# GpSimd operations that wait for the VectorE operation issued before them, and one PSUM tile for two stages of an attention and mixer kernel

## The chip, the cores and the metric

The kernel runs on one core of a Trainium2 chip. The time is the device time of one execution in microseconds (us). The engines of the core run side by side and are ordered among themselves by semaphores alone: TensorE (PE in the profile; its weight loads are PEld), VectorE (DVE), ScalarE (ACT), GpSimd (POOL) and SyncE (SP), which issues the transfers from and to the memory of the chip.

## What is computed

Rotary attention over 4 batches, 8 heads, 576 positions and a head size of 64, and behind it a token mixer and a channel mixer, all in float32. Cut to what matters:

```python
q_rot, k_rot = rotate(q), rotate(k)            # x1*cos - x2*sin, x1*sin + x2*cos
scores = matmul(q_rot, k_rot^T) / sqrt(64)
attn = exp(scores - max); attn = attn / (sum + 1e-9)
x = (attn @ v) with the heads side by side      # (4, 576, 512)
h = relu(x^T @ w_tok1) @ w_tok2                 # 576 -> 256 -> 576, over the positions
u = x + h^T
out = u + relu(u @ w_ch1) @ w_ch2               # 512 -> 1536 -> 512
```

The weights come as float64 (`moe_w_*`) and are turned on the chip into pairs of a high and a low part, each in the format in which TensorE multiplies fast; a product is then three matmuls (high by high, high by low, low by high).

## The kernel before

**Tasks and orders.** The kernel is written as tasks. `add` makes one: the engine, a cost estimate, a function that issues the instructions, what it depends on, and the buffers that it holds. A task can have alternatives on another engine. `Plan.run` hands the tasks out in one sequence, and each engine executes its own instructions in that sequence. Three calls of `run` follow each other. The first two take their sequence, with the choice of engines, from lists in the file (`ORDER1`: attention, the token weights and the token mixer of the first batch; `ORDER2`: the token mixers of the other three batches, the first transposes and the first group of channel weights). The third (the channel mixer and the remaining weights) makes its sequence by the plan's own clock: `start` estimates when a task could begin, `place` moves the clock and calls the task's function.

**Port tasks.** Some VectorE tasks have `port=True`: those that read two operands from SBUF or run in a fast mode from SBUF to SBUF. These are the steps of `f64_split` (lines 783 to 804: two ScalarE reads, a clamp at L787, a shift at L789, an OR at L791, a mask at L793, a product at L795, a sum at L797, then the high part at L803 and the low part at L804; L787, L795, L797 and L804 can also be GpSimd's), the split of the token mixer's input (`splits`, L865 and L867), and the rotation of the first pair of heads. In `start` the plan lets such a task begin only when its estimate of GpSimd's clock has passed, and in `place` it moves GpSimd's clock to the task's end. That is an estimate alone: no semaphore of the program orders the two engines for it.

**Attention.** The 16 pairs of heads are worked in a pipeline. For each pair (`prep`), GpSimd rotates k and q in three operations each (L470, L472, L476 on `w`, `uk`, `uq`); TensorE transposes the result (L505) and the copies go to `kt` and `qt` (L523). In `pair`, TensorE makes the scores (L649), VectorE takes each row's maximum on the way out of PSUM (L534, into `p`), ScalarE the exponentials (L546), TensorE transposes them (L675), ScalarE and VectorE copy them to `pt` (L685), TensorE multiplies by v (L698); the result goes through `oT` (L701) and a transpose (L727) to `X` (L732, L738), scaled by the reciprocal (L713) of a sum to which GpSimd adds 1e-9 (L710).

**PSUM.** In `attention` all eight banks are one tile `s` (128 x 8 x 512), from a pool that is opened in `attention` and closed behind the first `run`; `Banks` hands out its banks one by one and keeps for each the time at which it is free. `mixers` opens a second pool with eight tiles of one bank, `m0` to `m7`, and hands them out through `Slots`, all free at time 0.0. The second pool lies where the first one lay.

**Mixers.** `tokens` multiplies the split input by the token weights (L893), applies the ReLU and splits it (L898, L901), multiplies again (L915) and adds to `X` or its tails `XT` (L918). `splits` has two buffers `xs`, each freed by the L893 matmuls that read it. `up` transposes the result (L984) and splits it (L989, L990); `cm1` is the first channel product (L1010, L1012, L1014), `cm2` the second (L1037, L1039), in four groups of channel weights.

Of the kernel before, what the change touches and what calls it, by code (L numbers as in the profile page):

```python
# [9 lines left out]
F32 = mybir.dt.float32  # L10
# [5 lines left out]
PSUM = bass.MemoryType.PSUM  # L16
# [6 lines left out]
class Slots:  # L23


    def __init__(self, tiles, fifo=True):
        self.free = [(0.0, i, t) for i, t in enumerate(tiles)]
        self.fifo = fifo
        self.made = 0
        self.taken = 0  # L30
# [56 lines left out]
class Plan:  # L87


    def __init__(self):  # L90
        self.tasks = []
        self.made = 0
        self.given = False
        self.clock = {e: 0.7 for e in LAG}
        self.slack = SLACK
        self.mode = None

    def add(self, eng, dur, fn, deps=(), bufs=(), prio=0.0, alts=(), mode="full", port=False):
        t = Task()
        t.mode = mode  # L100
        t.port = port
        t.alts = [(eng, dur, fn)] + list(alts)
        t.deps = [d for d in deps if d is not None]
        t.bufs = list(dict.fromkeys(getattr(b, "buf", b) for b in bufs))
        for b in t.bufs:
            b.users += 1
        t.prio = prio
        t.end = None
        t.n = self.made = self.made + 1
        t.heirs = []  # L110
        self.tasks.append(t)
        return t
# [28 lines left out]
    def place(self, t, s, eng, dur, fn):  # L141
        end = s + dur
        for b in t.bufs:
            if b.held is None and isinstance(b.slots, Banks):
                sl = b.slots
                c = sl.pick(sl.free, b.two, self.clock["PE"])
                for i in c[1]:
                    del sl.free[i]
                i = c[1][0]
                b.held = (c[0], c[1], sl.tile[:, i:i + 2] if b.two else sl.tile[:, i])  # L150
            if b.held is None:
                b.held = min(b.slots.free)
                b.slots.free.remove(b.held)
                b.slots.taken += 1
        if fn:
            fn()
        else:
            end = -1e9
        t.end, t.eng = end, eng
        if eng == "PE":  # L160
            self.mode = t.mode
        self.clock[eng] = max(self.clock[eng], end)
        if eng == "DVE" and t.port:
            self.clock["POOL"] = max(self.clock["POOL"], end)
        for b in t.bufs:
            b.users -= 1
            b.end = max(b.end, end + LAG[eng])
            if not b.users and isinstance(b.slots, Banks):
                b.slots.free.update((i, b.end) for i in b.held[1])
            elif not b.users:  # L170
                b.slots.free.append((b.end,) + b.held[1:])
# [165 lines left out]
def rope_attention_mixer_kernel(ctx: ExitStack, tc: tile.TileContext, q, k, v, w_tok1, w_tok2, w_ch1, w_ch2, tab, out):  # L337
# [16 lines left out]
    NP = B * H // 2  # L354
    HP = H // 2
    P = 128
    plan = Plan()
    add = plan.add

    const = ctx.enter_context(tc.tile_pool(name="const", bufs=1))  # L360
    ident = const.tile([P, P], F32, name="ident")
    X = [const.tile([P, R, DM], F32, name=f"X{b}") for b in range(B)]
    XT = [const.tile([P, DM], F32, name=f"XT{c}") for c in range(B // 2)]
# [10 lines left out]

    def attention(ctx):
        pers = ctx.enter_context(tc.tile_pool(name="pers", bufs=1))
        psum = ctx.enter_context(tc.tile_pool(name="psum", bufs=1, space=PSUM))

        def slots(nm, n, shape, dt=F32, pool=pers, fifo=True):
            return Slots([pool.tile(shape, dt, name=f"{nm}{i}") for i in range(n)], fifo)  # L380
# [13 lines left out]
        lts = slots("lt", 2, [P, 4])  # L394
        rts = slots("rt", 2, [P, 4])
        nms = slots("nm", 8, [P, 2])
        banks = Banks(psum.tile([P, 8, 512], F32, name="s"), 8)

        for r0, r1 in ((0, 2), (2, R)):
            nc.scalar.dma_start(out=tabs[:, :, r0:r1], in_=tab[0:2, :, r0:r1].rearrange("a p r d -> p a r d"))  # L400
# [426 lines left out]
    def tok_weights(places):  # L827
        same = lambda x: x
        w1v = w_tok1[0:M, :].rearrange("(p r) f -> p (r f)", r=R)
        for i in range(2):  # L830
            pr = next(places)
            sb, t = stage(0, w1v[:, i * 512:(i + 1) * 512], pr)
            w1_done.extend(f64_split((sb, 512), [(w1h[:, 2 * i:2 * i + 2].rearrange("p r f -> p (r f)"),
                                                  w1l[:, 2 * i:2 * i + 2].rearrange("p r f -> p (r f)"), same)], [t], pr))
        pr = next(places)
        sb, t = stage(0, w_tok1[M:S, :], pr)
        _, t2 = stage(0, w_tok1[M:S, :], pr, o=1, sb=sb)
        w1_done.extend(f64_split((sb, FT), [(w1th, w1tl, same)], [t, t2], pr))
        for a in range(2):
            pr = next(places)  # L840
            sb, t = stage(0, w_tok2[a * P:(a + 1) * P, 0:M], pr)
            w2_done.extend(f64_split((sb, M), [(w2h[:, a, 0:M].rearrange("p (r s) -> p r s", r=R),
                                                w2l[:, a, 0:M].rearrange("p (r s) -> p r s", r=R),
                                                lambda x: x.rearrange("p (s r) -> p r s", r=R))], [t], pr))
        pr = next(places)
        sb, t = stage(0, w_tok2[0:P, M:S], pr)
        _, t2 = stage(TL, w_tok2[P:2 * P, M:S], pr, sb=sb)
        w2_done.extend(f64_split((sb, 2 * TL), [(w2h[:, :, M:S], w2l[:, :, M:S],
                                                 lambda x: x.rearrange("p (a s) -> p a s", a=2))], [t, t2], pr))
# [9 lines left out]
    def splits(b, rows, px):  # L859
        for r in rows:  # L860
            xb = Buf(xss if r < R else xts)
            src = X[b][:, r] if r < R else tail_of(b)
            hi = (lambda xb=xb: xb.t[:, 0]) if r < R else (lambda xb=xb: xb.t[0:TL])
            lo = (lambda xb=xb: xb.t[:, 1]) if r < R else (lambda xb=xb: xb.t[TL:P])
            c = lambda e, hi=hi, src=src: lambda: (e.copy if e is nc.scalar else e.tensor_copy)(out=hi(), in_=src)  # L865
            x = add("ACT", act(DM, True), c(nc.scalar), x_done[b], [xb], px, port=True, alts=[("DVE", dve2(DM), c(nc.vector))])
            f = lambda e, hi=hi, lo=lo, src=src: lambda: e.tensor_tensor(out=lo(), in0=src, in1=hi(), op=ALU.subtract)  # L867
            y = add("DVE", dve(DM), f(nc.vector), [x], [xb], px, port=True, alts=[("POOL", pool(DM), f(nc.gpsimd))] if r < R else [])
            split[b, r] = (xb, [x, y])
# [52 lines left out]
    KC = DM // P  # L922
    KF = FC // P

    def mixers(ctx):
        plan.slack = {"PE": 0.11, "ACT": 0, "DVE": 0, "POOL": 0, "SP": 0.18}
        wc = ctx.enter_context(tc.tile_pool(name="wc", bufs=1))
        psum = ctx.enter_context(tc.tile_pool(name="psum2", bufs=1, space=PSUM))
        m_ps = Slots([psum.tile([P, 512], F32, name=f"m{i}") for i in range(8)], False)
        FG = 3  # L930
        N = 4 * P
        W = FG * P
# [145 lines left out]
    with tc.manual_schedule():  # L1078
        with ExitStack() as c:
            banks = attention(c)  # L1080
            tok_weights(iter(AT["tok"]))
            for b in range(EARLY):
                tokens(b, banks)
            splits(EARLY, range(PRE), 9 * 4 * (EARLY + 1) + AT["pre"][0])
            for r in range(PRE):
                split[EARLY, r][0].users += 1
            plan.run(ORDER1)
        with ExitStack() as c:
            mixers(c)


# [44 lines left out]
```

## Time and profile before

| | |
|---|---|
| time, median of 3 runs | 599.67 us (599.59 to 599.69) |
| time of the profiled execution | 600.91 us |
| its span, first to last instruction | 599.1 us |
| busy in the span | PE 98%, DVE 65%, ACT 52%, POOL 51% |
| granted TensorE clock, mean | 0.993 |

The profile is that of one execution. Its time is the span and 1.8 us around it; it lies 1.24 us above the median of the three runs. An engine that is busy all the time in the profile is not at its peak, TensorE least of all: its matmuls overlap, and a matmul that is held up counts as busy. Where it waits shows best in the idle time of its weight loads (PEld), which run ahead of the matmuls.

### The profile page before, as it was taken

What the parts mean: (1) busy time and instruction counts of PE and PEld (TensorE: products, weight loads), DVE (VectorE), ACT (ScalarE), POOL (GpSimd) and SP (SyncE); (2) the same over time, 40 slices, a digit from 0 to 9 for tenths busy, and PEclk for the clock granted to TensorE, in tenths of its full rate; (3) what the DMA queues carried; (4) which work ended last, traced back from release to release, by engine and by line L of the source; (5) the groups of instructions that cost most, each with busy time, mean ns of one, the idle gap of its engine ahead of it and who ended that gap; (6) DMA issues with size and microseconds to landing.
All of it is one profiled execution on the core that took longest, in us unless ns stands there. A gap on an engine that the chain in (4) does not pass through costs nothing.

```text
span 599.1 us, 12781 instructions
## 1 busy us (share of the span) xinstructions
PE 589.1 (98%) x4865; PEld 464.4 (78%) x4865; DVE 390.2 (65%) x1129; ACT 309.7 (52%) x789; POOL 307.7 (51%) x257
## 2 busy tenths in 40 slices
PE   7999999999999999999999999999999999999997
PEld 6677676777777767677788888888888888888886
DVE  5998999999999987889956553345423443223232
ACT  2998989999999997265453432233202311110110
POOL 4999776977697722333666773277503750000000
PEclk7999999999999999999999999999999999999999
DMA  4524242132141101122312211122101100001123
GB/s 138 159 56 135 83 106 62 46 102 82 50 118 48 35 18 28 28 54 70 89 54 71 63 47 32 36 73 55 48 1 40 67 0 1 2 0 71 70 71 105
DMA packets 34093, 36.15 MB, mean 60 GB/s; under 512 B 13808, under 2 KB 27632, under 8 KB 34032
## 3 DMA queue, kind: packets, MB, share of 16 engines
q1 hardware_dynamic: 33200, 35.01, 20.3%
q8 instruction: 38, 0.62, 0.4%
q10 hardware_dynamic: 832, 0.33, 0.2%
q14 instruction: 23, 0.19, 0.1%
HBM read 30.61 MB, written 4.72 MB: 59 GB/s over the span
## 4 chain that ended last, share of the span: by engine, by line
PE 92%; DVE 6%; DMA 1%; issue 1%; ACT 0%; DVEq 0%
PE m L1010 25%; PE m L1037 25%; PE s L698 13%; PE s L649 11%; PE s L675 6%; PE m L915 2%; PE s L567 2%; PE s L505 2%; PE m L893 1%; PE s L893 1%; DVE p L534 1%; PE s L591 1%; PE s L727 1%; PE m L984 1%; DVE xs L867 1%
## 5 line engine op out<-in xcount | busy, mean ns | idle before, releaser
L1012 ACT ACTIVATE gh<-m 128x512 fp32r<-128x512 f32 (+1 forms) x60 | 33.3, 555 | 180.1 <-PE m L1010 180.1
L546 ACT ACTIVATE p<-p,nm 128x576 f32<-128x576 f32 x128 | 99.2, 779 | 5.7 <-DVE p L534 4.9
L1014 DVE SCALAR_TENSOR_TENSOR gl<-m,gh 128x512 fp32r<-128x512 f32 (+1 forms) x60 | 38.3, 638 | 97.8 <-ACT gh L1012 97.8
L1039 DVE TENSOR_TENSOR X<-m,X 128x512 f32<-128x512 f32 (+1 forms) x65 | 44.4, 683 | 68.4 <-PE m L1037 68.2
L1010 PE MATMUL m<-uh,c1h 128*128 128x512 f32 (+1 forms) x240 | 88.6, 369 | 0.0
L1010 PE MATMUL m<-ul,c1h 128*128 128x512 f32 (+1 forms) x240 | 88.3, 368 | 0.0
L1010 PE MATMUL m<-uh,c1l 128*128 128x512 f32 (+1 forms) x240 | 88.3, 368 | 0.0
L1037 PE MATMUL m<-c2l,gh 128*128 128x512 f32 (+1 forms) x219 | 84.6, 386 | 0.0
L1037 PE MATMUL m<-c2h,gh 128*128 128x512 f32 (+1 forms) x219 | 84.6, 386 | 0.0
L1037 PE MATMUL m<-c2h,gl 128*128 128x512 f32 (+1 forms) x219 | 84.5, 386 | 0.0
L698 PE MATMUL s<-pt,vraw 128*64 128x256 f32 (+1 forms) x640 | 84.4, 411 | 0.0
L649 PE MATMUL s<-kt,qt 64*128 64x288 f32 x512 | 83.1, 431 | 0.7 <-ACT kt L523 0.6
L795 POOL TENSOR_TENSOR fa<-fc,fa 128x512 f32<-128x512 f32 (+3 forms) x32 | 37.6, 1174 | 65.6 <-DVE fa L793 56.6
L698 PEld LDWEIGHTS s<-pt,vraw 128*64 128x64 f32 x640 | 43.2, 137 | 29.1 <-DVE p L534 1.7
L534 DVE TENSOR_SCALAR_CACHE_REDUCE p<-s,nm 128x288 f32<-128x288 f32 x128 | 61.3, 512 | 3.4 <-PE s L649 2.2
L685 ACT COPY pt<-s 128x320 f32<-128x320 f32 (+1 forms) x165 | 57.6, 408 | 8.6 <-PE s L675 7.5
L675 PEld LDWEIGHTS s<-ident,p 64*128 64x128 f32 x1152 | 45.9, 139 | 18.0 <-ACT p L546 6.3
L649 PEld LDWEIGHTS s<-kt,qt 64*128 64x128 f32 x512 | 52.2, 194 | 8.1 <-ACT kt L523 1.0
L534 DVE TENSOR_SCALAR_CACHE_REDUCE p<-s 128x288 f32<-128x288 f32 x128 | 54.0, 453 | 5.3 <-PE s L649 4.1
L675 PE MATMUL s<-ident,p 64*128 64x64 f32 x1152 | 52.1, 226 | 1.0 <-DVE pq L534 0.5
L1010 PEld LDWEIGHTS m<-uh,c1h 128*128 128x128 f32 x240 | 45.2, 188 | 7.8
L1010 PEld LDWEIGHTS m<-uh,c1l 128*128 128x128 f32 x240 | 45.2, 189 | 7.6
(133 smaller groups left out, 1074.4 us busy)
## 6 DMA issues: line engine op xcount, KB each, us to landing
stg<-in_moe_w_ch_dram SPq DMA_DIRECT2D x16, 384.0 KB, 3.2
stg<-in_moe_w_ch_dram SPq DMA_DIRECT2D x12, 512.0 KB, 3.7
vraw<-in_v_dram SPq DMA_DIRECT2D x16, 256.0 KB, 3.8
kraw<-in_k_dram SPq DMA_DIRECT2D x15, 256.0 KB, 3.1
qraw<-in_q_dram SPq DMA_DIRECT2D x15, 256.0 KB, 3.3
out_dram<-X SPq DMA_DIRECT2D x15, 256.0 KB, 2.3
stg<-in_moe_w_tok_dram SPq DMA_DIRECT2D x4, 512.0 KB, 4.6
kraw<-in_k_dram SPq DMA_DIRECT2D x32, 32.0 KB, 2.7
```

Of the source, the lines that this page charges most:

```text
L534: return lambda: nc.vector.tensor_scalar(out=p()[:, c * W2:(c + 1) * W2], in0=sb.t[:, 0:W2], scalar1=-D ** -0.5, scalar2=nm.t[:, 0:1] if c ...
L546: return lambda: nc.scalar.activation(out=p(), in_=p(), func=ACTF.Exp, bias=nm.t[:, 1:2], scale=-1.0, accum_out=l())
L649: nc.tensor.matmul(sbs[h].t[:, c0:c0 + W2], flat(qt.t)[halves[h], TL + j * P:TL + (j + 1) * P], flat(kt.t)[halves[h], TL * (1 - h) + u * W ...
L675: nc.tensor.transpose(xy[z].t[:, i * TL:(i + 1) * TL], pb.t[halves[z], c0:c0 + P], ident[halves[z], halves[z]])
L685: return lambda: e(out=pt[c].t[:, R * h:R * h + m, o + z * TL:o + (z + 1) * TL], in_=xy[z].t[:, 0:m * TL].rearrange("p (r s) -> p r s", r=m))
L698: nc.tensor.matmul(ab.t[halves[h], 0:w], vb.t[:, h, r, :], m, start=(r == 0), stop=(r == R))
L795: mul_ = lambda e: lambda: e.tensor_tensor(out=A(), in0=C(), in1=A(), op=ALU.mult)
L1010: nc.tensor.matmul(tb.t[:, 0:n], a, m, start=(i == 0), stop=(i == len(lst) - 1))
L1012: x = add("ACT", act(n), lambda f=f, tb=tb: nc.scalar.activation(out=gb.t[0][:, f, 0:n], in_=tb.t[:, 0:n], func=ACTF.Relu), [x], [tb, gb], ...
L1014: y = add("DVE", dve(n), lambda f=f, tb=tb: nc.vector.scalar_tensor_tensor(out=gb.t[1][:, f, 0:n], in0=tb.t[:, 0:n], scalar=0.0, in1=gb.t[ ...
L1037: nc.tensor.matmul(tb.t[:, 0:w], a, m, start=(i == 0), stop=(i == len(lst) - 1))
L1039: y = add("DVE", dve(w) + 0.08, lambda u=u, tb=tb, cols=cols, w=w: nc.vector.tensor_tensor(out=u[:, cols], in0=tb.t[:, 0:w], in1=u[:, cols ...
```

## The change

Two things are changed. First, the plan remembers the last VectorE instruction of a port task (`self.port`). The next GpSimd task that is placed gets a dependency on it, a semaphore wait in front of its first GpSimd instruction; then the memory is cleared, so only the first GpSimd task behind each such instruction waits. Nothing is added in the other direction. Second, the PSUM tile `s` is opened once, ahead of all stages, and `mixers` takes slices of it, with the times at which the attention's banks become free, in place of eight new tiles.

```diff
@@ class Plan
-    def __init__(self):
+    def __init__(self, tc):
...
+        self.tc = tc
+        self.port = None
@@ Plan.place
         if fn:
+            code = self.tc.nc.cur_bb.bb.instructions
+            k = len(code)
             fn()
+            if eng == "POOL" and self.port:
+                to = next(i for i in code[k:] if i.engine == mybir.EngineType.Pool)
+                self.tc.add_manual_dep(to, self.port.name, mybir.DependencyInfo(mybir.DependencyClass.Sync, mybir.DependencyReason.DATA), reason="port")
+                self.port = None
+            if eng == "DVE" and t.port:
+                self.port = code[-1]
         else:
             end = -1e9
@@ rope_attention_mixer_kernel
-    plan = Plan()
+    plan = Plan(tc)
...
+    psum = ctx.enter_context(tc.tile_pool(name="psum", bufs=1, space=PSUM)).tile([P, 8, 512], F32, name="s")
@@ attention
-        psum = ctx.enter_context(tc.tile_pool(name="psum", bufs=1, space=PSUM))
...
-        banks = Banks(psum.tile([P, 8, 512], F32, name="s"), 8)
+        banks = Banks(psum, 8)
@@ mixers
-    def mixers(ctx):
+    def mixers(ctx, banks):
...
-        psum = ctx.enter_context(tc.tile_pool(name="psum2", bufs=1, space=PSUM))
-        m_ps = Slots([psum.tile([P, 512], F32, name=f"m{i}") for i in range(8)], False)
+        m_ps = Slots([psum[:, i] for i in range(8)], False)
+        m_ps.free = [(banks.free[i], i, psum[:, i]) for i in range(8)]
@@ the call
-            mixers(c)
+            mixers(c, banks)
```

## Rows read from the trace of the kernel before

**Rows 1.** The page: busy time by engine; GpSimd's busy tenths in 40 slices.

```profile
PE 589.1 (98%) x4865; PEld 464.4 (78%) x4865; DVE 390.2 (65%) x1129; ACT 309.7 (52%) x789; POOL 307.7 (51%) x257
...
POOL 4999776977697722333666773277503750000000
```

**Rows 2.** Windows: stretch, busy PE, PEld, DVE, ACT, POOL (instructions), clock, DMA.

```profile
58.00:92.00 34.00, 33.38 (x444) 24.21 (x442) 32.08 (x116) 30.64 (x89) 27.20 (x21) 1.00 0.36 99
...
252.60:277.00 24.40, 22.96 (x125) 17.76 (x126) 22.02 (x38) 13.12 (x25) 7.17 (x6) 1.00 0.24 57
...
297.00:599.10 302.10, 298.73 (x1458) 249.95 (x1456) 125.07 (x212) 71.34 (x136) 111.94 (x87) 1.00 0.15 46
```

**Rows 3.** VectorE's timeline, five conversion steps: start, duration, both in us.

```profile
70.52 1.92 DVE L791 SCALAR_TENSOR_TENSOR fh<-stg,fa 128x512 uint32<-128x512 uint32 x1
...
75.64 2.08 DVE L791 SCALAR_TENSOR_TENSOR fh<-stg,fa 128x512 uint32<-128x512 uint32 x1
...
87.14 1.41 DVE L793 TENSOR_SCALAR fa<-fh 128x512 uint32<-128x512 uint32 x1
...
282.90 0.69 DVE L791 SCALAR_TENSOR_TENSOR fh<-stg,fa 128x512 uint32<-128x512 uint32 x1
...
284.11 0.42 DVE L793 TENSOR_SCALAR fa<-fh 128x512 uint32<-128x512 uint32 x1
```

**Rows 4.** GpSimd's timeline in the same stretch.

```profile
70.09 1.80 POOL L476 TENSOR_TENSOR uq<-uq,w 128x640 f32<-128x640 f32 x1
...
75.63 1.54 POOL L472 TENSOR_TENSOR uk<-kraw,tabs 128x640 f32<-128x640 f32 x1
...
80.72 1.56 POOL L476 TENSOR_TENSOR uk<-uk,w 128x640 f32<-128x640 f32 x1
...
86.72 1.54 POOL L472 TENSOR_TENSOR uk<-kraw,tabs 128x640 f32<-128x640 f32 x1 [2.93 <-PE s L505]
```

**Rows 5.** Waits of TensorE's weight loads, 69 to 92: us, times, longest.

```profile
PEld s L649 <- DVE p L534: 0.6, 1, 0.6
PEld s L675 <- DVE pq L534: 0.6, 1, 0.6
...
PEld s L649 <- DVE oT L701: 0.5, 1, 0.5
...
PEld s L567 <- ACT p L546: 0.4, 1, 0.4
```

**Rows 6.** TensorE's timeline: the transposes that read the rotated k.

```profile
86.07 0.49 PE L505 MATMUL s<-ident,uk 64*128 64x64 f32 x10
```

**Rows 7.** TensorE's timeline, end of attention and 23 us behind it.

```profile
252.18 0.40 PE L915 MATMUL s<-rs,w2l 128*64 128x512 f32 x1
...
253.48 0.74 PE L893 MATMUL m<-xs,w1h 128*128 128x512 f32 x2 [0.91 <-DVE XT L918]
...
275.24 0.39 PE L893 MATMUL m<-xs,w1l 128*128 128x512 f32 x1
...
276.19 0.73 PE L893 MATMUL m<-xs,w1h 128*128 128x512 f32 x2 [0.56 <-DVE ul L990]
```

**Rows 8.** Waits of TensorE's weight loads, 252 to 277.

```profile
PEld m L893 <- DVE XT L918: 1.4, 1, 1.4
PEld m L893 <- DVE ul L990: 1.0, 1, 1.0
```

**Rows 9.** The line L867 on VectorE: ns min/median/max, starts, shapes.

```profile
L867 DVE TENSOR_TENSOR xs<-X,xs x11: 677/693/1500, 232.5 to 283.5; 128x512 fp32r<-128x512 f32 x11
```

**Rows 10.** Timeline, VectorE and GpSimd from 240 on.

```profile
240.19 0.22 DVE L793 TENSOR_SCALAR fa<-fh 128x128 uint32<-128x128 uint32 x1
...
240.55 0.46 POOL L795 TENSOR_TENSOR fa<-fc,fa 128x128 f32<-128x128 f32 x1 [0.91 <-DVE fa L793]
```

**Rows 11.** Timeline around 274, GpSimd and VectorE.

```profile
273.80 1.19 POOL L795 TENSOR_TENSOR fa<-fc,fa 128x384 f32<-128x384 f32 x1 [5.64 <-DVE fa L793]
...
274.04 1.50 DVE L867 TENSOR_TENSOR xs<-X,xs 128x512 fp32r<-128x512 f32 x1
```

## The prediction

> **What bounds the kernel now.** I read the page first, then the windows by stage, then the waits of TensorE's weight loads, then the timelines at the places that these point to. On the page TensorE is busy for 98% of the span and nothing else for more than 65% [rows 1], so the reader is to look for the few places where TensorE stands still. The windows divide them. From 297 us on TensorE is busy for 298.73 of 302.10 us [rows 2], and no matmul of that stretch waits for another engine: what is changed there is hidden as long as weights arrive in time. Before it, TensorE shares the bound with VectorE, which is busy for 32.08 of 34 us between 58 and 92 and for 22.02 of 24.40 us between 252.6 and 277 [rows 2]. Here a late VectorE operation becomes a hole in TensorE.
>
> Three VectorE operations of the first of these stretches are far too long: an L791 that takes 0.69 us elsewhere takes 1.92 and 2.08, an L793 that takes 0.42 takes 1.41 [rows 3]. Beside each, GpSimd's timeline has an operation on SBUF that is under way when it starts or starts with it: L476 from 70.09 to 71.89, L472 from 75.63 to 77.17, L472 from 86.72 to 88.26 [rows 4]. The VectorE operation ends 0.56, 0.55 and 0.29 us behind GpSimd's end, so it did its work only then. Excess: 1.92 - 0.69 = 1.23, 2.08 - 0.69 = 1.39, 1.41 - 0.42 = 0.99 us. In the program's sequence each of these GpSimd operations, or one in front of it in GpSimd's queue, stands behind the VectorE operation that it holds up; it got ahead because its inputs were ready while VectorE was late.
>
> **The seam: one PSUM tile.** The last matmul on the old tile starts at 252.18, the first on `m` at 253.48, released by the last addition that reads the old tile (XT, L918) [rows 7]. Its inputs were split before. With slices of one tile it has to wait only for the readers of its own bank, and the times handed to `mixers` make it take the bank that was free first. From 297 us on 1458 matmuls start in 302.1 us, 0.21 us apart [rows 2]; the two starts at the seam are 1.30 apart. Gain 1.30 - 0.21 = 1.1 us; bounds are TensorE's idle 0.91 [rows 7] and the idle 1.4 of its weight loads [rows 8]. It lasts, because what follows hangs on these matmuls: they free `xs`, ScalarE and VectorE refill it, TensorE goes on. Moving the tile ahead of the other pools, the slices and the argument `tc` issue no instruction; which bank is taken changes nothing else, since a bank that was just freed is later in the list than one of the old ones either way. If a bank's reader were late instead, the gain would shrink by that lateness, down to 0.
>
> **The waits, at 69 to 92 us.** VectorE gets back the three excesses, 3.6 us in all, if GpSimd starts behind it. TensorE gets back only what it lost. Its weight loads wait three times for a VectorE operation queued behind one of the three long ones: 0.5 (oT, behind the first), 0.6 (pq, behind the second), 0.6 (p, behind the third) [rows 5]. Each is shorter than the excess in front of it, so each can vanish. Behind the first stands a wait of 0.4 for ScalarE's exponentials [rows 5], which I take to remain: 0.1 is left of it. Sum 0.1 + 0.6 + 0.6 = 1.3 us. Bounds: 0 (GpSimd late in place of VectorE, below) and 3.6 (all of the excess, if matmuls that count as busy were also held up).
>
> What is late next is GpSimd. The L476 at 70.09 starts behind the L791 at about 70.52 + 0.69 + 0.14 = 71.35 (0.14 is the handover from VectorE's end at 240.41 to GpSimd's start at 240.55 [rows 10]): 1.3 us later. The next rotation, at 74.13, stands behind the L791 of 75.64: 75.64 + 0.69 + 0.14 = 76.5, 2.3 us later, and with it all that is queued behind it on GpSimd up to the L476 that ends at 80.72 + 1.56 = 82.28 [rows 4], now 84.6. Its reader is the transpose L505 at 86.07 [rows 6], which comes 0.7 us earlier by then (0.1 + 0.6): 85.4. The margin falls from 3.8 to 0.8 us, and the cost is zero. The next operation, at 86.72, waits for L505 anyway [rows 4] and starts some 0.3 later. SyncE's loads of the next k and q wait for the same operations, and move by the same 2 us; they are read one pair later. Without that cover each further us of GpSimd costs one us of TensorE. The other waits of attention (19 in its sequence) push GpSimd back by some 2 us at a few places and not at all where VectorE was done already; GpSimd is idle for 6.8 of the 34 us [rows 2], which takes up such delays. I take 0 for them; the upper bound is one margin missed by as much as the deferral above, 2.3 us.
>
> **The waits, at 252 to 277 us.** The same again: L867 on `xs` takes 0.69 in the middle and 1.50 at most [rows 9]; the longest starts at 274.04, with GpSimd's L795 in front of it from 273.80 [rows 11] and later in the sequence. TensorE's next hole is at 276.19, released by the VectorE operation queued right behind it; the starts are 0.95 apart in place of 0.21, so 0.74 us is lost [rows 7] (the weight loads' 1.0 [rows 8] is the upper bound), less than the excess 1.50 - 0.69 = 0.81. Gain 0.7 us; lower bound 0. What GpSimd does here are the conversions of channel weights, needed from 297 us on; delays of some us are hidden there.
>
> **The waits, from 297 us.** GpSimd's conversions start up to some 1.5 us later each. TensorE has no hole that they could fill or make: GpSimd's row of slices is empty for the last seven [rows 1], which are 105 us, so its work ends long before the last group of weights is used. 0 us; if the cover were gone, at most the one deferral of 1.5 us per group.
>
> **The sum.** 1.1 + 1.3 + 0.7 = 3.1 us: 600.91 becomes 597.8 for the profiled execution. That one lies 1.24 above the median; the gain is taken from the median: 599.67 - 3.1 = 596.6 us. Its own range, with the bounds of the terms that are nearest (seam 0.9, 79 to 92 us 1.0, 276 us 0.4; and 1.4, 1.7, 1.0), is 595.6 to 597.4.
>
> **The rivals.** *The conflict moves.* GpSimd now starts just as a VectorE operation ends, and the next VectorE port operation, if it comes within GpSimd's 1.0 to 1.8 us and stands later in the sequence, is held up in its place; nothing was added against that. For it: VectorE has rows of conversions without a pause behind 252.6 us; against it: at 70.52 and 75.64 what follows on VectorE reads PSUM (L701, L534), and the next conversion is 3 us away or more. If half of the waits' 2.0 us is lost so: 599.67 - 1.1 - 1.0 = 597.6. The Trainium skill (SBUF — State Buffer, Who interferes with whom) has the rule for it: the pair of ports that VectorE and GpSimd share is an exclusive lock, whoever starts first keeps it for its whole instruction, and the order of issue decides who blocks. The three ends above agree (0.56, 0.55 and 0.29 us behind GpSimd's [rows 3, 4]); by that rule a wait in one direction alone moves the loss to VectorE's next such operation, and the sum would be the 597.6 of this rival where the terms above give 596.6.
>
> *Only the seam.* VectorE gets its time back, but TensorE's holes have a second cause just behind (ScalarE, as at the 0.4, or GpSimd): 599.67 - 1.1 = 598.6. Against it: the rows name VectorE for 1.7 us of holes in the first stretch.
>
> *The change doesn't do it.* The first matmul on the slices still waits for L918 as its bank's reader, and the GpSimd operations were not what VectorE waited for: 599.7. Against it: both rows name their releaser.
>
> *Slower: rotations come late.* The 0.8 us of margin at the L505 of 86.07 is the smallest that I worked out, and it hangs on the handover of 0.14. If waits cost GpSimd 0.6 us each instead, in front of the three that matter here, the rotated k is 1.8 us later than forecast, 1.0 past the margin; the pipeline of pairs has more such places, and from about four of them on (4 x 1.0 against 3.1) the kernel is slower. At six: 596.6 + 6.0 = 602.6. Against it: GpSimd's idle time between.
>
> **The chances.** Forecast 0.52, the conflict moves 0.20, only the seam 0.15, no effect 0.05, slower 0.08. A difference under 0.2% (1.2 us) can't be told from none here, so faster means below 598.47: forecast and the moved conflict wholly, and of "only the seam", at 598.6 with 0.3 to either side, a third: 0.52 + 0.20 + 0.05 = 0.77. Same: the rest of it and no effect, 0.15. The range of 8 in 10 takes in the forecast, the moved conflict and half of the seam alone: 595.4 to 598.8.
>
> **What would show it.** Right: L791 and L793 near 70, 75 and 87 us take 0.7 and 0.4; the three waits of rows 5 on VectorE are gone; the first L893 starts 0.2 us behind the last L915; no hole at 276; the last matmul chain from L1010 on is as long as before. Wrong: L505 waits for GpSimd's L476; long VectorE port operations at new places; a first L893 that waits for a VectorE L918 again.

## The result

The changed kernel takes **595.16 us** (median of 4 runs, 594.76 to 595.85) against 599.68 us (599.59 to 600.73) of the kernel before: ratio **0.9919, interval 0.9904 to 0.9935**. It is 4.5 us faster; 3.1 were forecast. The profiled execution takes 595.85 us with a span of 594.1 us, 5.0 us less than the span before. The lines that the prediction names stand 10 lower now (L791 is L801, L893 is L903), and the tile `m` is called `s`.

The page, busy time by engine:

```profile
PE 587.1 (99%) x4865; PEld 464.7 (78%) x4865; DVE 385.0 (65%) x1129; ACT 309.3 (52%) x789; POOL 302.0 (51%) x257
```

VectorE and GpSimd do the same instructions as before in 5.2 and 5.7 us less [rows 1]: what went is time in which the one or the other was held up. VectorE's timeline, the three operations that answer to the long ones of [rows 3]:

```profile
70.29 0.69 DVE L801 SCALAR_TENSOR_TENSOR fh<-stg,fa 128x512 uint32<-128x512 uint32 x1
...
74.66 0.69 DVE L801 SCALAR_TENSOR_TENSOR fh<-stg,fa 128x512 uint32<-128x512 uint32 x1
...
85.28 0.42 DVE L803 TENSOR_SCALAR fa<-fh 128x512 uint32<-128x512 uint32 x1
```

They took 1.92, 2.08 and 1.41 in the kernel before. GpSimd's timeline, which answers to [rows 4]:

```profile
71.14 1.56 POOL L486 TENSOR_TENSOR uq<-uq,w 128x640 f32<-128x640 f32 x1 [1.36 <-DVE fh L801]
...
75.47 1.55 POOL L480 TENSOR_TENSOR w<-kraw,tabs 128x640 f32<-128x640 f32 x1 [0.83 <-POOL w L480]
...
81.64 1.54 POOL L486 TENSOR_TENSOR uk<-uk,w 128x640 f32<-128x640 f32 x1
...
85.86 1.55 POOL L482 TENSOR_TENSOR uk<-kraw,tabs 128x640 f32<-128x640 f32 x1 [1.17 <-PE s L659]
```

Each waiting operation now starts 0.13 to 0.17 us behind VectorE's end (70.29 + 0.69 = 70.98, start 71.14; 75.35, start 75.47; 85.70, start 85.86). (The brackets of the second and the last name another releaser; the starts just behind VectorE's end show the added wait.) The waits of TensorE's weight loads from 66 to 90 us, for [rows 5]:

```profile
PEld s L685 <- ACT pt L695: 0.5, 1, 0.5
PEld s L515 <- issue: 0.4, 1, 0.4
PEld s L577 <- ACT pt L695: 0.4, 1, 0.4
PEld s L685 <- ACT p L556: 0.4, 1, 0.4
PEld s L601 <- ACT p L556: 0.4, 1, 0.4
```

No VectorE wait is left. The one for ScalarE in front of the scores (L567, now L577) is still there with 0.4, though the profile now names another ScalarE operation as its releaser (the copy to `pt`, not the exponentials). TensorE's timeline at the transposes of [rows 6], at the seam and at the old hole of 276.19 [rows 7]:

```profile
84.20 0.48 PE L515 MATMUL s<-ident,uk 64*128 64x64 f32 x10
...
249.47 0.39 PE L925 MATMUL s<-rs,w2l 128*64 128x512 f32 x1
249.70 0.62 PE L903 MATMUL s<-xs,w1h 128*128 128x512 f32 x2
...
271.04 0.39 PE L903 MATMUL s<-xs,w1l 128*128 128x512 f32 x1
271.27 0.61 PE L903 MATMUL s<-xs,w1h 128*128 128x512 f32 x2
```

The rotated k is ready at 81.64 + 1.54 = 83.18, 1.0 us ahead of its reader at 84.20; at the seam two starts are 0.23 us apart in place of 1.30; the hole at 276.19 is gone.

**Where the time came from.** Both kernels start the same 4865 matmuls in the same order, so their starts can be lined up one by one. The difference grows in a few steps and is flat in between:

| starts before, us | forecast | after | tile alone | waits alone |
|---|---|---|---|---|
| 72 to 73 | 0.1 | 0.77 | 0 | 0.77 |
| 80 to 82 | 0.6 | 0.87 | 0 | 0.87 |
| 89 | 0.6 | 0.84 | 0 | 0.84 |
| 253, the seam | 1.1 | 1.20 | 1.22 | 0 |
| 262 to 270 | 0 | 0.29 | 0 | 0.29 |
| 276 | 0.7 | 0.86 | 0 | 0.86 |
| from 297 | 0 | 0 | 0 | 0 |
| sum, with drifts under 0.03 | 3.1 | 4.83 | 1.19 | 3.60 |

The seam and the hole at 276 each consist of the gap itself (1.07 and 0.73) and some 0.12 more: in the kernel before, the second matmul behind each gap starts 0.34 us after the first, and not 0.23 (the pairs of [rows 7] take 0.74 and 0.73 us, those of the kernel after 0.62 and 0.61). The first 18 us are left out of the table: there the starts of any two executions differ, of the same kernel too (below). Of the missing 1.7 us, 1.2 lie in attention, 0.3 between 262 and 270, and 0.1 to 0.2 each at the seam and at 276.

**Why the rows showed too little.** One pair of windows tells it. Both hold the same 294 matmuls, from just in front of the first conflict to just behind the third. Before:

```profile
69.00:92.03 23.03, 22.41 (x294) 15.66 (x292) 21.95 (x75) 20.15 (x58) 19.54 (x16) 1.00 0.43 117
```

After:

```profile
68.80:89.30 20.50, 20.50 (x294) 14.88 (x292) 18.82 (x75) 19.59 (x58) 16.65 (x15) 1.00 0.44 128
```

The stretch is 2.53 us shorter, but TensorE's idle time before was only 23.03 - 22.41 = 0.62 us. The other 1.9 us were counted as busy: matmuls already under way in the record, held up by a missing operand. The timeline of before at the first conflict, the scores and the exponentials' reader behind it:

```profile
72.19 1.47 PE L649 MATMUL s<-kt,qt 64*128 64x288 f32 x4
73.58 1.20 PE L567 MATMUL s<-kt,qt 64*64 64x288 f32 x16
```

And after:

```profile
71.96 0.70 PE L659 MATMUL s<-kt,qt 64*128 64x288 f32 x4
72.60 1.20 PE L577 MATMUL s<-kt,qt 64*64 64x288 f32 x16
```

The four score matmuls took 1.47 us and take 0.70. These 0.77 us are the whole first step, all of it inside busy time. The weight loads run ahead and were idle for 0.5 us there [rows 5], of which the prediction left 0.1. The third conflict is alike; the same seven score matmuls, before and after:

```profile
88.19 2.03 PE L649 MATMUL s<-kt,qt 64*128 64x288 f32 x7
...
86.32 1.19 PE L659 MATMUL s<-kt,qt 64*128 64x288 f32 x7
```

That is 0.84 us, again the whole step, with TensorE busy all the while. So the sentence ahead of the prediction, that TensorE's waits show best in the idle time of its weight loads, does not hold here.

### The profile page after: what moved, and what is told of

Same layout as the page of the kernel before. It is cut to its first block, busy times and chain, and to the rows that moved or that the text cites. A ratio compares the mean times of both kernels' runs of the same rounds, so it can differ in the third digit from the quotient of the medians.

```text
span 594.1 us, 12793 instructions
## 1 busy us (share of the span) xinstructions
PE 587.1 (99%) x4865; PEld 464.7 (78%) x4865; DVE 385.0 (65%) x1129; ACT 309.3 (52%) x789; POOL 302.0 (51%) x257
## 4 chain that ended last, share of the span: by engine, by line
PE 96%; DVE 1%; ACT 1%; DMA 0%; issue 0%; DVEq 0%; ACTq 0%
PE s L1020 25%; PE s L1047 25%; PE s L708 13%; PE s L659 11%; PE s L685 7%; PE s L925 5%; PE s L903 4%; PE s L515 2%; PE s L577 2%; PE s L601 1%; PE s L994 1%; PE s L737 1%; ACT p L556 1%; DVE p L544 1%; DMA tabs<-in_tab_dram 0%; DVE w L480 0%
## 5 line engine op out<-in xcount | busy, mean ns | idle before, releaser
L1024 DVE SCALAR_TENSOR_TENSOR gl<-s,gh 128x512 fp32r<-128x512 f32 (+1 forms) x60 | 38.3, 638 | 98.2 <-ACT gh L1022 98.2
L1020 PE MATMUL s<-uh,c1h 128*128 128x512 f32 (+1 forms) x240 | 88.7, 369 | 0.0
L1020 PE MATMUL s<-ul,c1h 128*128 128x512 f32 (+1 forms) x240 | 88.4, 368 | 0.0
L1020 PE MATMUL s<-uh,c1l 128*128 128x512 f32 (+1 forms) x240 | 88.3, 368 | 0.0
L1049 DVE TENSOR_TENSOR X<-s,X 128x512 f32<-128x512 f32 (+1 forms) x65 | 44.4, 684 | 67.6 <-PE s L1047 67.4
L1047 PE MATMUL s<-c2l,gh 128*128 128x512 f32 (+1 forms) x219 | 84.7, 387 | 0.0
L1047 PE MATMUL s<-c2h,gh 128*128 128x512 f32 (+1 forms) x219 | 84.6, 387 | 0.0
L1047 PE MATMUL s<-c2h,gl 128*128 128x512 f32 (+1 forms) x219 | 84.6, 386 | 0.0
L1020 PEld LDWEIGHTS s<-uh,c1h 128*128 128x128 f32 x240 | 45.3, 189 | 7.8
L1020 PEld LDWEIGHTS s<-uh,c1l 128*128 128x128 f32 x240 | 45.3, 189 | 7.6
```

The source lines that it names most:

```text
L1020: nc.tensor.matmul(tb.t[:, 0:n], a, m, start=(i == 0), stop=(i == len(lst) - 1))
L1024: y = add("DVE", dve(n), lambda f=f, tb=tb: nc.vector.scalar_tensor_tensor(out=gb.t[1][:, f, 0:n], in0=tb.t[:, 0:n], scalar=0.0, in1=gb.t[ ...
L1047: nc.tensor.matmul(tb.t[:, 0:w], a, m, start=(i == 0), stop=(i == len(lst) - 1))
L1049: y = add("DVE", dve(w) + 0.08, lambda u=u, tb=tb, cols=cols, w=w: nc.vector.tensor_tensor(out=u[:, cols], in0=tb.t[:, 0:w], in1=u[:, cols ...
```

## The experiments

The times of a group stand beside the kernel before on the same chip (600.35 us in the first group of four, 600.04 in the second, 600.14 in the third). The waits are counted in the program's sequence: 19 in attention (1 to 19), 9 in the second sequence (20 to 28), 30 behind it.

**e1_tile, the tile alone.**

```diff
-            if eng == "POOL" and self.port:
-                to = next(i for i in code[k:] if i.engine == mybir.EngineType.Pool)
-                self.tc.add_manual_dep(to, self.port.name, ...)
-                self.port = None
-            if eng == "DVE" and t.port:
-                self.port = code[-1]
```

> The PSUM tile without any of the waits. Theory (the two parts add up, and the seam is worth the gap between its two matmuls): the first L893 starts 0.2 us behind the last L915 in place of 1.3, the rest stays, 1.1 us faster than before. Rival (the gain of the seam is real only with the waits, because without them VectorE's queue at 257 to 276 us eats it): under 0.4 us faster.

Measured: 598.97 us, ratio 0.9979 (0.9971 to 0.9988). The only step is the seam's, 1.2 us, 1.07 of it in front of the first matmul.

**e2_waits, the waits alone.**

```diff
...
-        m_ps = Slots([psum[:, i] for i in range(8)], False)
-        m_ps.free = [(banks.free[i], i, psum[:, i]) for i in range(8)]
+        psum = ctx.enter_context(tc.tile_pool(name="psum2", bufs=1, space=PSUM))
+        m_ps = Slots([psum.tile([P, 512], F32, name=f"m{i}") for i in range(8)], False)
```

> All 58 waits with the eight tiles of before. Theory: 2.5 us from 69 to 92 us and 1.1 from 257 to 277, 3.6 us faster than before; seam gap of 1.3 us unchanged. Rival (parts overlap): under 3.0 us, with the missing part in the second stretch.

Measured: 596.49 us, ratio 0.9937 (0.9925 to 0.9949). The seam is as before (first matmul on `m` released by VectorE's L928 after 0.91 us); the other steps are those of the table. The two parts add up: 0.21% and 0.63% alone, 0.81% together; in steps 1.19 and 3.60 us, and 4.83.

**e3_three, three waits of attention alone, eight tiles.**

```diff
...
+                self.waits += 1
+                if self.waits in (3, 4, 5):
...
```

> Only the three waits in front of the L476 at 70.09, the L470 at 74.13 and the L472 at 86.72, nothing else of the change. Theory (three held VectorE operations cost TensorE more than its idle rows said): 2.5 us faster than before, the same 2.5 as the whole set of waits has up to 92 us. Rival (it is the sum of many small hold-ups over all 19 waits of attention): 1.3 us or less.

Measured: 598.85 us, ratio 0.9969 (0.9957 to 0.9981). The starts up to 92 us come 2.5 us earlier, as in the kernel after, so these three waits hold the whole gain of attention. Then 0.6 us are given back at 96 to 97 us. VectorE and GpSimd there (line numbers 3 above those of after):

```profile
92.33 1.27 DVE L806 TENSOR_SCALAR fa<-fh 128x512 uint32<-128x512 uint32 x1
...
92.04 1.28 POOL L808 TENSOR_TENSOR fa<-fc,fa 128x512 f32<-128x512 f32 x1
```

The mask that takes 0.42 us elsewhere takes 1.27, behind a GpSimd operation that started 0.29 us in front of it. Neither the kernel before nor the kernel after has this conflict: the three waits made VectorE earlier, and it met the next operation of GpSimd. In the kernel after, the wait nr 6 stands on that operation.

**e4_second, the waits 20 to 28 alone, eight tiles.** The same edit with `20 <= self.waits <= 28`.

> Only the nine waits of the second sequence (257 to 293 us). Theory: 1.1 us faster than before, all of it between 261 and 277 us, nothing in front. Rival (the conflict moves to the next VectorE operation of the same stretch): under 0.4 us.

Measured: 598.80 us, ratio 0.9977 (0.9968 to 0.9986). Steps of 0.19 us at 262, 0.10 at 270 and 0.86 at 276, nothing in front and nothing behind.

**e9_one, the disputed first term by itself.** Eight tiles, `self.waits == 3`.

> The kernel before (eight tiles) with one wait alone: the one on the GpSimd rotation that started at 70.09 in front of VectorE's L791 of 70.52. It tells the disputed first term by itself. Theory (the weight loads' idle row of 0.5 understates what TensorE lost there, since matmuls that were held up count as busy, and the wait of 0.4 for ScalarE is no remainder): the matmuls behind 73 us start 0.7 to 0.8 us earlier than in the kernel before. The two conflicts behind it stay, since the next rotation still starts in front of the L791 of 75.64. Time some 0.7 us under the kernel before. Rival (the prediction's term): 0.1 us, no change that can be told. Rival (the gain is given back at the next conflict, since GpSimd is later there and VectorE earlier): 0.7 us at 73, nothing left at 92.

Measured: 599.40 us, ratio 0.9987 (0.9978 to 0.9996): 0.74 us. The starts step by 0.77 us at 72 to 73 and keep that to the end. TensorE's scores at that place and VectorE's next conflict (line numbers 3 above those of after):

```profile
71.29 0.70 PE L662 MATMUL s<-kt,qt 64*128 64x288 f32 x4
...
73.98 2.04 DVE L804 SCALAR_TENSOR_TENSOR fh<-stg,fa 128x512 uint32<-128x512 uint32 x1
```

The first conflict alone cost 0.77 us and not 0.1, while the second stays as long as it was.

**e5_zero, the times of the banks left out.**

```diff
-        m_ps.free = [(banks.free[i], i, psum[:, i]) for i in range(8)]
```

> The kernel after, with one line less: the mixers' list of free banks has all eight at time zero in their order, so that the first L893-kind matmuls (L903 of after) take bank 0, and not the bank that was read last-but-longest. Bank 0 is still being read then by one of VectorE's additions L928, which in the kernel after runs from 248.85 to 250.14, while the first L903 starts at 249.70. Theory (a bank's own readers decide): the first L903 waits for that addition and starts about 0.5 us later than in the kernel after, the rest of the seam's 1.07 stays gained: time 595.7, and only the step at the seam changes. Rival (one tile is enough, whichever bank comes first): no difference, 595.2. Rival (the tile as a whole is tracked): the seam's 1.07 is lost again, 596.2.

Measured: 596.39 us, ratio 0.9935 (0.9923 to 0.9947). TensorE at the seam:

```profile
248.71 0.40 PE L925 MATMUL s<-rs,w2l 128*64 128x512 f32 x1
249.42 0.73 PE L903 MATMUL s<-xs,w1h 128*128 128x512 f32 x2 [0.32 <-DVE X L928]
```

The gap is 0.71 us in place of 0.23, and the releaser is an addition to `X`, not the later one to `XT`: the readers of its own bank decide. The starts lose 0.60 us there against the kernel after, 0.48 in the gap and 0.12 at the second matmul, and no other start moves. So one tile alone gives half of the seam's 1.20, the choice of the bank the other half.

**e8_five, five of the 58 waits, with the one tile.** `self.waits in (3, 4, 5, 6, 24)`.

> The kernel after with 5 of its 58 waits: those on the GpSimd operations that were at 70.09, 74.13, 86.72 and 92 us, and the one that was at 273.80. One PSUM tile as in the kernel after. Theory (four conflicts between 70 and 92 us, one at 274, and the seam are nearly the whole gain): 2.5 + 0.75 + 1.07 of the kernel after's gain, without some 0.4 us of small steps between 261 and 270 us: 595.2 + 0.4 = 595.6. Rival (without the other waits the earlier TensorE meets new conflicts, as it did at 96 us where the wait there was missing): 596.5 or more, with a VectorE operation of over 1 us at a place where neither kernel has one.

Measured: 596.40 us, ratio 0.9937 (0.9924 to 0.9951), an interval that overlaps that of the kernel after. The starts lose 0.19 us at 258, 0.10 at 266 and 0.05 at 271 against the kernel after, nothing else: 53 waits together are worth 0.3 us by the trace. The medians, of different chips, lie 1.2 us apart; no run tells why.

**e6_late1 and e6_late4, waits that cost GpSimd more.** In front of each waiting operation stand one, or four, more GpSimd operations, with the wait on the first. One took 0.40 us as measured, four took 1.83. They compute nothing that is used.

```diff
+            if eng == "POOL" and self.port:
+                for _ in range(1):
+                    self.tc.nc.gpsimd.tensor_tensor(out=self.scr, in0=self.scr, in1=self.scr, op=ALU.mult)
             fn()
```

> The kernel after, and in front of each GpSimd operation that waits for VectorE one more GpSimd operation on a scratch tile, 128x128 f32, about 0.46 us as L795 of this shape takes; the wait stands on the extra one. So each of the 58 waits delays GpSimd by 0.46 us more. The smallest margins of the kernel after are 1.0 us for the rotated q at 73.73 (one wait in front), 1.0 for the rotated k at 84.20 (two waits in front, 0.92), 0.5 for the rotated q at 136.53 (one wait). Theory (GpSimd's lateness is covered up to these margins): within 0.3 us of the kernel after, 595.2 to 595.6. Rival (waits that cost GpSimd 0.6 in place of 0.14 make the kernel slow, as the slower rival of the prediction has it): some 1 us at each of four to six places, 599 to 601.

> The same with four extra operations, 1.84 us for each wait. Theory (covered up to the margins, one for one behind them): L515 waits for GpSimd at 73.73 (1.84 - 1.0 = 0.8), at 84.20 (3.7 in all, less 1.0 and the 0.8 already lost: 1.9), at 136.53 (1.3), at 149.23 (0.7): 4.7 us more than the kernel after, about 600, with 598 to 602 as the range since the places shift. Rival (idle time of GpSimd takes it up): 595.2 to 596. Rival (every one of the 19 waits of attention costs its 1.84 less 0.5): over 610.

Measured with one: 597.11 us, ratio 0.9949 (0.9934 to 0.9964). In attention no start moves by 0.1 us. Two places behind it do, against the kernel after: 0.85 us at 271 and 0.52 at 285 to 290. GpSimd, VectorE and TensorE at the first of them (line numbers 5 above those of after):

```profile
268.25 1.01 POOL L819 TENSOR_TENSOR c1l<-fh,c1h 128x384 fp32r<-128x384 f32 x1
...
268.47 1.01 DVE L808 TENSOR_SCALAR fa<-fh 128x384 uint32<-128x384 uint32 x1
...
271.21 0.72 PE L908 MATMUL s<-xs,w1h 128*128 128x512 f32 x2 [0.54 <-DVE ul L1005]
```

A mask of 0.35 us is held for 1.01, three operations later `ul` is late, and TensorE stands. This is not GpSimd missing its reader, as the expectation had it, but the conflict that moves: 0.4 us of shift puts it on the path. With four: 628.43 us, ratio 1.0470 (1.0451 to 1.0489), far out of the expected 598 to 602. Of the four margins that were worked out three hold well and the second is a third short (0.77, 1.27, 1.34 and 0.71 us for 0.8, 1.9, 1.3 and 0.7), but attention loses 12 us in all, at more places than these. The waits of TensorE's weight loads from 60 to 250 us for the rotated k and q:

```profile
PEld s L520 <- POOL uk L491: 3.6, 4, 1.2
PEld s L520 <- POOL uq L491: 2.8, 2, 1.6
```

The other 20 us are lost behind it. At the one place shown here VectorE's conversions wait for GpSimd's, and TensorE for what is queued behind them on VectorE. TensorE's timeline in e6_late4 and one window of it:

```profile
288.63 1.22 PE L908 MATMUL s<-xs,w1h 128*128 128x512 f32 x2 [2.98 <-DVE ul L1005]
...
290.07 1.05 PE L908 MATMUL s<-xs,w1h 128*128 128x512 f32 x2
...
290.93 0.63 PE L908 MATMUL s<-xs,w1l 128*128 128x512 f32 x1
...
288.70:294.40 5.70, 5.70 (x14) 4.51 (x15) 3.73 (x7) 2.54 (x5) 5.23 (x10) 0.52 0.26 80
```

and VectorE ahead of it:

```profile
286.81 0.56 DVE L806 SCALAR_TENSOR_TENSOR fh<-stg,fa 128x384 uint32<-128x384 uint32 x1 [1.73 <-POOL c1l L819]
```

**e10_late_att, the one extra operation in attention's 19 waits alone.** The same edit, with `self.waits < 20`.

> The kernel after with the extra GpSimd operation of 0.4 us in front of the 19 waiting operations of attention alone, none behind 252 us. Theory (margins of 1.0, 1.0 and 0.5 us cover 0.4 to 0.8 us in attention; what the variant with 0.4 us at all 58 waits lost was lost at 271 and 285 us, where a later GpSimd meets the next VectorE conversion): same as the kernel after, steps of the matmuls under 0.2 us up to 252 us, 0.3 us at most in all. Rival (the lateness of attention is handed on to the second stretch): again 0.7 us at 271 us and 0.6 at 285 to 290.

Measured: 595.12 us, ratio 0.9915 (0.9901 to 0.9928), the same as the kernel after beside it. No step of 0.1 us behind 18 us. So attention takes 0.4 us more for each wait at no cost, and what e6_late1 loses is lost by the nine waits behind 252 us.

**e7_reverse, waits in both directions.**

```diff
+            if eng == "DVE" and t.port and self.back:
+                to = next(i for i in code[k:] if i.engine == mybir.EngineType.DVE)
+                self.tc.add_manual_dep(to, self.back.name, ...)
+                self.back = None
...
+            if eng == "POOL":
+                self.back = code[-1]
```

> The kernel after, and VectorE's operations that share the way to the memory wait for the last GpSimd operation in front of them in the sequence too, so that no such operation of either engine is ever under way beside one of the other that stands in front of it. What it tells is what the held VectorE operations that remain in the kernel after (0.1 to 0.8 us over at six places between 256 and 285 us) cost. Theory (a wait costs VectorE what being held cost it): within 0.4 us of the kernel after. Rival (being held costs more than a wait, since the held operation ends 0.3 to 0.6 us behind GpSimd's end): 0.5 us or more faster. Rival (VectorE now stands behind GpSimd operations that have not even begun, 1.75 us each at 229.8 and 238.2): 1 to 3 us slower, with steps of the matmuls there.

Measured: 595.63 us, ratio 0.9920 (0.9906 to 0.9933), no difference to the kernel after beside it (0.9915). The page:

```profile
PE 586.4 (99%) x4865; PEld 463.7 (78%) x4865; DVE 378.5 (64%) x1129; ACT 309.6 (52%) x789; POOL 300.8 (51%) x257
```

VectorE is busy for 6.5 us less than in the kernel after, for the same instructions: so much of being held is left there, and the starts of TensorE's matmuls don't move by 0.2 us anywhere behind 18 us against those of the kernel after. What is left lies off the path.

**e11_after, the kernel after again, beside the three.**

> The kernel after itself, beside the three others on the same chip, as the measure for them: 595.2, the ratio to the kernel before 0.992. Nothing else is asked of it.

Measured: 595.12 us, ratio 0.9915 (0.9902 to 0.9929). No kernel of the study beats it by more than can be told.

## Why the prediction was right and wrong

**The direction, the places and the mechanism held.** All three VectorE operations went to 0.69, 0.69 and 0.42, the three waits of [rows 5] are gone, the seam is 0.23 us, the hole at 276 is gone, the last group of channel weights is as long as before. (Each held operation ended with less than its own time left behind GpSimd's end, so "did its work only then" goes too far; below.) e1 and e2 show that tile and waits work apart from each other.

**The seam (forecast 1.1, measured 1.20, of it 1.07 in the gap that was priced) was right**, and so was its condition: with a bank whose reader is later, 0.6 us of it are lost (e5).

**The step that failed is the term of attention, 1.3 us; it measured 2.48.** It was sized by the idle time of the weight loads, 0.5 + 0.6 + 0.6, less 0.4 of the first for ScalarE's exponentials "which I take to remain". Both halves were wrong. The wait for ScalarE does remain in the profile, but it stands in front of other weight loads (L567) than the one for VectorE (L649) and costs no start; e9 measured the first term alone at 0.77 and not 0.1. And the idle rows of the second and third conflict (0.6 each) are smaller than what the starts lost (0.87 and 0.84): at the third the whole loss is booked as busy time of the held matmuls, at the second TensorE's matmuls show 0.46 us of idle time (in front of L675 at 79.80) for 0.87. The measured losses are 0.77 of 1.23, 0.87 of 1.39 and 0.84 of 0.99 us of VectorE's excess: the upper bound of 3.6 us, which the prediction named for just this case, was as near as its own value. That bound didn't enter the range: for its low end the term was taken at 1.7, the three idle rows in full, and the result lies 0.24 us under the range. A range with the excess as the far end of this term would have held it.

**The second stretch (forecast 0.7) was short by 0.45.** The hole at 276 gave 0.86, as its second matmul was late too. Two more steps, 0.19 at 262 and 0.10 at 270, come from small conflicts between 255 and 270 us that the prediction put at nothing; e4 shows both. In the kernel before, VectorE's L867 at 257.57, 258.72 and 265.69 take 1.12, 1.40 and 1.13 us in place of 0.69, and L787 at 267.21 takes 1.16 in place of 0.35, each beside a GpSimd operation; in the kernel after all four take their own time.

**From 297 us: 0, as forecast.** **GpSimd's lateness: 0, as forecast**; the margin at the transposes of k came out at 1.0 us for the 0.8 worked out, and e10 shows 0.4 us more per wait still covered, with 0.5 us of that margin left (ready at 82.45 + 1.56 = 84.01, read at 84.50).

**The rivals.** *Only the seam* and *The change doesn't do it* fall with e1 and e2. *The conflict moves* happens, but not at its price: VectorE's held time fell by 5.2 us only and 6.5 remain, off the path (e7). In the kernel after, operations are held at new places, such as the L799 at 263.18 and 281.78 (0.80 us each; 0.36 and 0.43 in e7). It becomes costly as soon as the timing shifts: 0.6 us in e3, 1.4 in e6_late1. The Trainium skill (SBUF — State Buffer, Who interferes with whom) says that of the two engines the one that issues first keeps the shared ports for its whole instruction and the other blocks fully. The held operations of e3 and e6_late1 agree in that they end behind GpSimd's end, by 0.28 and 0.22 us. What the rule can't tell is whether anybody waits for the one that is blocked. *Slower: rotations come late* was put at 0.6 us for each wait in place of 0.14. Its sum counts the 0.6 in full where the forecast already held 0.14 of it (three times 0.46 is 1.4, not 1.8), and it adds up three waits. At 0.54 (0.14 + 0.40) attention loses nothing (e10): the extra operations at two waits took 0.5 us of the margin and not 0.8, since the second wait starts from VectorE's end again, whatever the first one cost. At four extra operations it is far slower than its 602.6 (e6_late4).

What stays open: which of the held operations between 255 and 270 us makes which of the two small steps, and of e6_late4's 33 us all but the places named above.

## What to carry to other kernels

A stall of the busiest engine isn't safely sized by its idle time, nor by that of its weight loads: count how many matmuls are started in a window, or compare the time of one group of matmuls with that of the same form elsewhere (1.47 against 0.70 us here), and keep the releaser's whole excess as the far end of the range. Two engines that hold each other up are worth ordering where the held one is on the path; here five waits of 58 do nearly all of it, but each gain shifts the timing, and the next pair of operations must be covered too. Where two stages share a buffer, one tile with slices lets each slice wait for its own readers, and which slice is taken first is worth a look.

## What the runs showed of the hardware

**A held operation needs less than its whole time behind its holder.** The mask of 0.42 us ended 0.28 us behind GpSimd's end in e3 (93.32 to 93.60), the one of 0.35 us 0.22 us behind it in e6_late1 (269.26 to 269.48), the OR of 0.69 us 0.55 both times in the kernel before, and the mask of 0.42 us 0.29 [rows 3, 4]. GpSimd's spans are rough in a profile, so the difference may be one of the record.

**A long stall costs TensorE its clock on top.** In e6_late4 TensorE stood for 2.98 us, and in the window from 288.70 to 294.40 behind it the granted clock is 0.52, that is the level of 1.2 GHz: the L908 matmuls from 290.07 to 291.35 start 0.43 us apart, where those of the kernel after at 271.04 are 0.23 apart. By an estimate the 14 matmuls of that window lost 14 x 0.2 = 2.8 us more. Two more stalls of that run, of 3.05 and 2.30 us, are followed by a low clock too (0.57 from 361.90 to 365.90, 0.72 from 396 to 402). In the windows of the kernel before, with holes of up to 0.9 us, it is 1.00 [rows 2].

**The first 18 us differ from one execution to the next.** Between two executions of the kernel after, the starts differ by 0.44 to 0.48 us from there on; between the kernel before and e9 by 0.9 ahead of the first edit. That is of the size of the spread of one kernel's times (1 to 2 us), and why the steps are read behind it. The clock has a part in it: from 12 to 14 us the granted clock is 0.50 in the kernel before and 0.97 in e9, and the same 19 score matmuls take 4.46 us there (from 11.45) and 3.70 here (from 11.32). TensorE had stood still thereabouts in both, for 1.13 us up to 7.77 and for 1.20 us up to 7.82. (The profile of the kernel after reads 1.00 there, but its 19 matmuls take 4.36 us, so that reading is in doubt.)
